# A block-local attention and a token/channel mixer in one kernel: the order in segment 0, batch 1's transposed x, and when later x is loaded

## The chip, the cores and the metric

The kernel runs on one core of a Trainium2 chip. The metric is the time of one execution on the device, in microseconds (us), as the median of several runs. Three runs of the kernel before took 849.24, 851.77 and 852.95 us, with a median of 851.77.

Five engines work side by side, each through its own queue of instructions, in order: TensorE (PE: matmuls, with its weight loads shown apart as PEld), VectorE (DVE), ScalarE (ACT), GpSimd (POOL) and SyncE (SP), which here only issues the transfers (DMAs). An instruction that must wait holds up all that stands behind it in its queue.

## The reference

For 8 batches with 8 heads, 576 tokens and a head size of 64, an attention within chunks of 64 tokens makes x, and a mixer works on it:

```
s = 1/sqrt(64) * q_chunk @ k_chunk^T
p = exp(s - max(s)); p = p / (sum(p) + 1e-9)
x = (p @ v_chunk), heads side by side        # 8 x 576 x 512

h = relu(x^T @ w_tok1) @ w_tok2              # 576 -> 256 -> 576, over tokens
u = x + h^T
out = u + relu(u @ w_ch1) @ w_ch2            # 512 -> 1536 -> 512, over channels
```

The four weights arrive as 64-bit floating-point numbers, and all else is float32.

## The kernel before

**Layout.** The mixer's channel part works with channels on the 128 partitions and tokens on the free axis. Eight batches of 576 tokens make 4608 columns, cut into nine blocks of N = 512 columns. Block k (k = 0 to 8) thus holds the last 64·k columns of batch k-1 and the first 512-64·k of batch k. The attention works with tokens on the partitions, in tiles of 128 tokens: nine tiles for a pair of batches, where the fifth is shared half and half by the two. So x has to be transposed on its way into a block.

**Precision.** A matmul operand is split into a high part and a low part in a reduced float32 format (F32R), and each product takes three matmuls (high·high, low·high, high·low). This is why names come in pairs: `xh`/`xl` for x, `uh`/`ul` for a block of u, `gh`/`gl` for the hidden layer behind the relu, `rh`/`rl` for the token layer behind its relu.

**Weights.** There are 29 weight pieces: 5 of the token mix, then `c1` and `c2` pieces of the channel mix, 12 each. Each is fetched as raw 64-bit words (`raw`, 512 KB for a channel piece, L116) and converted on the chip. ACT makes two reads of the words (L133, L134, issued by `prepare()`, which also fetches the raw words three pieces ahead) and a cast to the high part `kept` (L205); DVE does the rest: clamp, sign, shift, add, and the split of the low part (L211). `convert(n)` takes n **conversion steps** from this list; a channel piece takes five DVE steps. All pieces stay on the chip once they are converted.

**Segments and steps.** The channel mix runs in segments (block, first piece, end): (0, 0..8), (1, 0..12), (0, 8..12), then blocks 2 to 8 over 0..12. Segment 0 is the first of these and does only eight of block 0's twelve pieces, since the weights are still being converted; what it has summed is parked in memory (the part stores and loads). A **step** f does `ch1` (12 matmuls, L556, into one of two PSUM banks `ps_c`), the relu into `gh` on ACT (L564) and `gl` on DVE (L565), and then `ch2` of the step before (12 matmuls into the four sums `acc`, L587).

**Attention.** In some steps (a table sets which: 0, 2, 4 and 6 in segment 0) an `attention` runs. It works on two neighbouring tiles: the older one, whose weights are finished, and the newer one, whose scores begin. In order: ACT copies the older tile's transposed weights `pf` to `pt` (L346); PE makes the newer tile's scores from `qk` (L295) and the older tile's product with `v` (L307), into one tile of two PSUM banks; `qk` and `v` of a later tile are loaded; DVE takes the maximum and subtracts it (L268, L271), ACT takes the exponential `pr` (L275); DVE scales the older product to `x` (L386). Then `pr` is transposed by a way through memory: DVE transposes 32x32 blocks (`blocks`, L318), a store writes them to memory (`far`, L323), and four loads bring them back as `pf` (L329). Last, the older tile's x is split into `xh` and `xl`, and goes the same way as `pr`: one transposition, one `far` store and loads (L329) into `xt`, the transposed x of a block. The loads that belong to a block after the next are put on a list, `late`.

**Start.** The first five tiles (block 0) run ahead of the segments, with matmuls in full float32 and transposes on PE; in front of each tile's next scores stand conversion instructions (`PREPARE`, `FIRST_FILL`).

**Turn.** At the last step in front of a new block ("turn"), PE does `tok1` (two halves, L475, each in a bank of `ps_c`, with relu to `rh`/`rl`), `ch2` of the step before, and `tok2` (L538) for four column blocks m of 128 channels; then DVE adds the transposed x (`u` = sum + `xt`, L543), ACT casts to `uh` (L547), DVE makes `ul` (L548); then comes `ch2` of the last step. Column blocks 0 and 1 take the two banks of `ps_c`, 2 and 3 share one tile of two banks (`two`). At the end of the turn SP issues all `late` loads of x, one after the other.

**What sets the order.** In segment 0 all engines work in the order of the code. From segment 1 on PE and SP keep the order of the code, while ACT and DVE are ordered by a scheduler. SP issues all transfers, in the order of the code.

## Time and profile before

| | |
|---|---|
| median of the runs | 851.77 us |
| profiled execution, its own time | 855.66 us |
| its span (first to last instruction) | 853.7 us |
| granted TensorE clock, mean | 0.967 |
| PE busy | 788.4 us, 92% of the span |
| PEld (weight loads) | 635.6 us, 74% |
| DVE | 378.1 us, 44% |
| ACT | 214.7 us, 25% |
| POOL | 85.6 us, 10% |
| bytes moved | 89.88 MB |

How to read what is quoted below: the page cuts the span into 40 equal slices, and a digit is the busy share of a slice in tenths. In a row of waits stand the engine, the operand and line that waited, the engine, operand and line it waited for, and then total us, number of times and longest. A row of windows has its bounds, its length, and the busy time (with the number of instructions) of PE, PEld, DVE, ACT and POOL, then the granted clock (1 is full speed), the share of DMA time and GB/s. A row of the timeline has the start in us, the duration, the engine, the line and the operation; "x4" are four in a row, counted as one, and the bracket at the end gives how long the engine stood idle before it and for whom. A row with a line number, an operand and "x12" behind two times is the same, cut to one operand.

### The profile page before, as it was taken

The numbers are of one execution on the slowest core, as the hardware profiler recorded it, in microseconds if no ns is written. First come the engines' busy times: TensorE is split into PE (matmuls) and PEld (weight loads), VectorE is DVE, ScalarE is ACT, GpSimd is POOL, SyncE is SP. The second block draws the span as 40 slices with busy tenths as digits, with TensorE's granted clock in tenths as the row PEclk, the third lists the DMA queues.
The fourth block names the chain that finished last, engine by engine and source line by source line (L and its number), as shares of the span: only waits on it lengthen the run. The fifth ranks groups of instructions, "written<-read, shape, count | busy, mean of one in ns | idle before, by whom it ended". The sixth has DMA issues, their size and how long they took to land.

```text
span 853.7 us, 13430 instructions
## 1 busy us (share of the span) xinstructions
PE 788.4 (92%) x5552; PEld 635.6 (74%) x5552; DVE 378.1 (44%) x660; ACT 214.7 (25%) x361; POOL 85.6 (10%) x74
## 2 busy tenths in 40 slices
PE   6885578799999999999999999899999999999998
PEld 4464456688888888878888888778887787887886
DVE  4788784853544433634344334425352324114112
ACT  4545442321231222212322221212211211111010
POOL 0000000200200100211020102100030102003100
PEclk9997789899999999999999999899999999999999
DMA  9636551432452432154315331534043102001001
GB/s 356 233 105 191 186 186 55 136 100 79 145 173 80 132 112 81 66 165 137 112 40 155 110 100 44 167 109 133 27 137 118 51 1 92 1 1 37 13 1 49
DMA packets 67371, 89.88 MB, mean 105 GB/s; under 512 B 7984, under 2 KB 40240, under 8 KB 67312
## 3 DMA queue, kind: packets, MB, share of 16 engines
q1 hardware_dynamic: 67312, 89.05, 31.8%
q8 instruction: 43, 0.70, 0.4%
q14 instruction: 16, 0.13, 0.0%
HBM read 61.10 MB, written 27.00 MB: 103 GB/s over the span
## 4 chain that ended last, share of the span: by engine, by line
PE 79%; DMA 8%; DVE 8%; ACT 3%; issue 1%; SPq 1%; ACTq 0%; DVEq 0%
PE acc L587 33%; PE ps_c L556 30%; PE ps_t L475 5%; PE ps_t L538 5%; DMA raw<-in_wc 3%; DMA far<-blocks 2%; PE ps_sv L307 2%; PE ps_sv L295 2%; DMA v<-in_v 2%; DVE u L543 1%; SPq L329 1%; DVE wtop L150 1%; PE ps_t L517 1%; DMA pf<-far 1%; DVE wtop L157 1%
## 5 line engine op out<-in xcount | busy, mean ns | idle before, releaser
L587 PE MATMUL acc<-gh,kept 128*128 128x512 f32 x864 | 282.0, 408 | 5.0 <-DVE kept L211 5.0
L556 PE MATMUL ps_c<-uh,kept 128*128 128x512 f32 x864 | 270.3, 394 | 0.0
L565 DVE SCALAR_TENSOR_TENSOR gl<-ps_c,gh 128x512 fp32r<-128x512 f32 x108 | 74.6, 691 | 347.9 <-ACT gh L564 347.9
L587 PEld LDWEIGHTS acc<-gh,kept 128*128 128x128 f32 x864 | 165.2, 195 | 42.7 <-DVE kept L211 5.4
L556 PEld LDWEIGHTS ps_c<-uh,kept 128*128 128x128 f32 x864 | 162.9, 189 | 36.9 <-DVE kept L211 0.4
L587 PE MATMUL acc<-gl,kept 128*128 128x512 f32 x432 | 173.6, 402 | 1.6 <-DVE gl L565 1.6
L556 PE MATMUL ps_c<-ul,kept 128*128 128x512 f32 x432 | 169.7, 393 | 0.0
L564 ACT ACTIVATE gh<-ps_c 128x512 fp32r<-128x512 f32 x108 | 64.5, 597 | 316.4 <-PE ps_c L556 316.4
L587 PEld LDWEIGHTS acc<-gl,kept 128*128 128x128 f32 x432 | 83.9, 194 | 21.9 <-DVE gl L565 2.0
L556 PEld LDWEIGHTS ps_c<-ul,kept 128*128 128x128 f32 x432 | 81.5, 189 | 18.8
L404 POOL TENSOR_TENSOR xl<-x,xh 128x512 fp32r<-128x512 f32 x28 | 36.4, 1299 | 456.7 <-ACT xh L403 445.5
L598 POOL TENSOR_TENSOR o<-o,ul 128x512 f32<-128x512 f32 x32 | 43.3, 1383 | 250.2 <-DVE o L596 157.7
L538 PE MATMUL ps_t<-kept,rh 128*128 128x448 f32 (+7 forms) x224 | 49.5, 314 | 6.2 <-DVE u L543 6.2
L307 PE MATMUL ps_sv<-v,pt 64*64 64x64 f32 x992 | 22.3, 232 | 34.9 <-ACT pt L346 34.9
L307 PEld LDWEIGHTS ps_sv<-v,pt 64*64 64x64 f32 x992 | 19.0, 146 | 36.2 <-ACT pt L346 35.9
L538 PEld LDWEIGHTS ps_t<-kept,rh 128*128 128x128 f32 x224 | 37.0, 189 | 9.3 <-DVE u L543 7.8
L275 ACT ACTIVATE pr<-pr 128x512 f32<-128x512 f32 x36 | 22.7, 631 | 68.7 <-DVE pr L271 66.5
L346 ACT COPY pt<-pf 128x512 f32<-128x512 f32 x31 | 19.2, 619 | 74.0 <-DMA pf<-far 71.7
L547 ACT CAST uh<-u 128x512 fp32r<-128x512 f32 x32 | 19.9, 621 | 69.2 <-DVE u L543 69.2
L543 DVE TENSOR_TENSOR u<-ps_t,xt 128x512 f32<-128x512 f32 x32 | 22.0, 689 | 31.9 <-PE ps_t L538 31.7
L475 PE MATMUL ps_t<-xh,kept 128*128 128x512 f32 x112 | 35.0, 393 | 0.0
L538 PE MATMUL ps_t<-kept,rl 128*128 128x448 f32 (+7 forms) x112 | 34.7, 310 | 0.0
(74 smaller groups left out, 606.4 us busy)
## 6 DMA issues: line engine op xcount, KB each, us to landing
qk<-in_qk SPq DMA_DIRECT2D x36, 512.0 KB, 4.3
far<-blocks SPq DMA_DIRECT2D x63, 256.0 KB, 2.1
raw<-in_wc SPq DMA_DIRECT2D x24, 512.0 KB, 5.5
v<-in_v SPq DMA_DIRECT2D x36, 260.0 KB, 4.1
out<-o SPq DMA_DIRECT2D x32, 256.0 KB, 2.0
pf<-far SPq DMA_DIRECT2D x124, 64.0 KB, 2.0
xt<-far SPq DMA_DIRECT2D x96, 64.0 KB, 2.0
xt<-far SPq DMA_DIRECT2D x64, 32.0 KB, 1.8
```

The lines of the kernel that those rows point to most:

```text
L275: nc.scalar.activation(out=pr, in_=pr, func=AF.Exp, scale=1.0 / float(D) ** 0.5)
L307: nc.tensor.matmul(ps[c * CH:(c + 1) * CH, a, (NHP + hp) * D:(NHP + hp + 1) * D], lhsT=t["pt"][a * CH:(a + 1) * CH, hp, c * CH:(c + 1) * C ...
L404: nc.gpsimd.tensor_tensor(out=xl, in0=t["x"], in1=xh.bitcast(F32), op=ALU.subtract)
L475: nc.tensor.matmul(ps, lhsT=lhsT, rhs=rhs, start=(n == 0 and q == 0), stop=(n == len(mt) - 1 and q == len(terms) - 1),)
L538: nc.tensor.matmul(ps[:, at:at + n], lhsT=lhsT[:, cols], rhs=rhs, start=(q == 0), stop=(q == len(terms) - 1),)
L543: nc.vector.tensor_tensor(out=u.rearrange("p (i c) -> p i c", c=BK), in0=ps.rearrange("p (i c) -> p i c", c=BK), in1=xt(k)[:, :, m], op=AL ...
L547: nc.scalar.copy(out=uh[:, m], in_=u)
L556: nc.tensor.matmul(ps, lhsT=weights["c1", f][:, wi, k * P:(k + 1) * P], rhs=u[ui][:, k], start=(k == 0 and q == 0), stop=(k == NDT - 1 and ...
L564: nc.scalar.activation(out=gh, in_=ps, func=AF.Relu)
L565: nc.vector.scalar_tensor_tensor(out=gl, in0=ps, scalar=0.0, in1=gh.bitcast(F32), op0=ALU.max, op1=ALU.subtract)
L587: nc.tensor.matmul(accs[e], lhsT=weights["c2", f][:, wi, e * P:(e + 1) * P], rhs=g[gi], start=(first and q == 0), stop=(end and q == 2),)
L598: nc.gpsimd.tensor_tensor(out=o, in0=o, in1=ul, op=ALU.add)
```

## The change

The arithmetic of x, u and the output stays as it is, except that block 1 gets its x by other matmuls. The change moves and replaces work at these places:

1. *Start.* `PREPARE` goes from two pieces a tile to one, and `END_FILL` from (3, 3, 2) to (3, 2, 2). The first attention takes two conversion steps along. A second identity matrix in F32R, `ident_r`, is made by one ACT cast.
2. *Segment 0, order in a step.* Before, a step ran `prepare` and six conversion steps ahead of its relu and `prepare` and four behind its attention. Now the relu comes first, then the attention, then twice `prepare` and five steps (`STEP_FILL`).
3. *Attention.* The conversion step inside it (one in segment 0) stands ahead of the `far` transposition. `attn_load`, the loads of `qk` and `v`, is moved from right behind the matmuls to behind the `far` store and `pf` loads.
4. *Block 1's x.* At the turn to block 1, x of batches 0 and 1 is added within PSUM by matmuls against an identity matrix, nine for each column block (`tok2` with k == 1). So `u` is the PSUM tile itself, and the three full tiles of batch 1 that are done in segment 0 and only serve block 1 are split, but not stored to `far` or loaded to `xt`. The half tile shared by both batches is stored as before, and loaded later.
5. *PSUM of `tok2`.* Column blocks 0 to 2 use the banks of `ps_c` in turn, and block 3 has the attention's tile alone.
6. *Late x.* The loads of the `late` list are no more issued at the end of the turn, but one by one (four transfers each) at steps 0, 3, 5, 6, 8, 10 and 11 of the next segment (`LATE`), and the shared tile's behind them.
7. One more buffer for `u`, `o` and `back` (5 in place of 4).

```diff
 WARM_T = (6, 2, 0, 0, 0)
 FIRST_FILL = (2, 2, 2, 2, 2)
-PREPARE = (0, 2, 2, 2, 2)
-END_FILL = (3, 3, 2)
-STEP_FILL = (6, 4)
+PREPARE = (0, 1, 1, 1, 1)
+END_FILL = (3, 2, 2)
+STEP_FILL = 5
+LATE = (0, 3, 5, 6, 8, 10, 11)
  
 
...
     ident = const.tile([P, P], F32, name="ident")
     make_identity(nc, ident)
     ctx.enter_context(tc.manual_schedule(engines={nc.sync.engine}))
+    ident_r = const.tile([P, P], F32R, name="ident_r")
+    nc.scalar.copy(out=ident_r, in_=ident)
 
...
                 part = slice(rows.start, rows.start + n * BK)
                 if wait and k > b:
                     late.append((tiles[t]["x"], k, at, n, part))
-                else:
+                elif k > 1:
                     far_in(tiles[t]["x"], xt(k)[:, at:at + n], part)
                 rows = slice(part.stop, rows.stop)
                 first += n
...
             if not n:
                 continue
             terms = []
+            if k == 1:
+                for t, rows, j in mix_tiles(b):
+                    first, end = max(j * P, lo), min(j * P + rows.stop - rows.start, lo + n)
+                    if first >= end:
+                        continue
+                    rows = slice(rows.start + first - j * P, rows.start + end - j * P)
+                    to = ps[:, at + first - lo:at + end - lo]
+                    for x in (tiles[t]["x"],) if b == 0 else (tiles[t]["xh"], tiles[t]["xl"]):
+                        terms.append((to, x[rows, cols], (ident if b == 0 else ident_r)[rows, rows]))
+            to = ps[:, at:at + n]
             for t in range(NT1):
                 if b == 0:
-                    terms.append((rs[b][t], tops["t2", t][:, lo:lo + n]))
+                    terms.append((to, rs[b][t][:, cols], tops["t2", t][:, lo:lo + n]))
                 else:
-                    terms += [(rs[b][t][ri], weights["t2", t][:, wi, lo:lo + n]) for wi, ri in THREE]
-            for q, (lhsT, rhs) in enumerate(terms):
+                    terms += [
+                        (to, rs[b][t][ri][:, cols], weights["t2", t][:, wi, lo:lo + n]) for wi, ri in THREE
+                    ]
+            for q, (to, lhsT, rhs) in enumerate(terms):
                 nc.tensor.matmul(
-                    ps[:, at:at + n], lhsT=lhsT[:, cols], rhs=rhs,
-                    start=(q == 0), stop=(q == len(terms) - 1),
+                    to, lhsT=lhsT, rhs=rhs, start=(q == 0), stop=(q == len(terms) - 1),
                 )
-        u = pool.tile([P, N], F32, tag="o", name="u", bufs=4)
-        nc.vector.tensor_tensor(
-            out=u.rearrange("p (i c) -> p i c", c=BK), in0=ps.rearrange("p (i c) -> p i c", c=BK),
-            in1=xt(k)[:, :, m], op=ALU.add,
-        )
+        u = ps
+        if k > 1:
+            u = pool.tile([P, N], F32, tag="o", name="u", bufs=5)
+            nc.vector.tensor_tensor(
+                out=u.rearrange("p (i c) -> p i c", c=BK), in0=ps.rearrange("p (i c) -> p i c", c=BK),
+                in1=xt(k)[:, :, m], op=ALU.add,
+            )
         nc.scalar.copy(out=uh[:, m], in_=u)
         nc.vector.tensor_tensor(out=ul[:, m], in0=u, in1=uh[:, m].bitcast(F32), op=ALU.subtract)
 
-    def ch1(u, f, fill=0):
+    def ch1(u, f):
         while ("c1", f) not in weights:
             convert(1)
         ps = ps_c1.tile([P, N], F32, tag="c1", name="ps_c1")
...
                     ps, lhsT=weights["c1", f][:, wi, k * P:(k + 1) * P], rhs=u[ui][:, k],
                     start=(k == 0 and q == 0), stop=(k == NDT - 1 and q == 2),
                 )
-        if fill:
-            prepare()
-            convert(fill)
         gh, gl = [pool.tile([P, N], F32R, tag=tag, name=tag) for tag in ("gh", "gl")]
         nc.scalar.activation(out=gh, in_=ps, func=AF.Relu)
         nc.vector.scalar_tensor_tensor(
...
         if j is not None:
             attn_t(j)
         attn_both(i, j)
-        if j is not None and k + 1 < len(order):
-            attn_load(order[k + 1])
         if i is not None:
-            attn_p(i, fill)
+            attn_p(i)
         if j is not None:
             attn_o(j)
+        convert(fill)
         if i is not None:
             attn_far(i)
             attn_z(i)
-        if j is not None:
+        if j is not None and k + 1 < len(order):
+            attn_load(order[k + 1])
+        if j in second[:3]:
+            attn_split(j)
+        elif j is not None:
             attn_end(j)
             for b in range(1, B):
                 if j in [t for t, _, _ in mix_tiles(b)] and (b % 2 == 0 or j % NTILE != 4):
                     attn_x(b, j, wait=True)
 
+    half = []
+
     def ready():
+
         attn_stack(first[4], range(1, 2))
-        tiles[first[4]]["x"] = far_out(tiles[first[4]]["x"], "far_s")
-        attn_x(0, first[4])
+        half.append(far_out(tiles[first[4]]["x"], "far_s"))
 
     def split(i):
         split_high(i)
...
                 half_low.append(half_kept[:, c])
 
     rs, us = {0: r}, {0: block_u()}
-    attention(0)
+    attention(0, 2)
     for m in range(NDT):
         tok2_first(r, m, us[0], ps_acc.tile([P, N], F32, tag="acc", name="ps_t2"))
         convert(END_FILL[2])
     start_ps.close()
-    done, pend, accs = 1, None, []
+    done, pend, accs, owed = 1, None, [], []
     after = None
     for seg, (k, lo, hi) in enumerate(SEGMENTS):
         slots = SLOTS.get((k, lo), SLOTS[3 - (k + 1) % 2] if 2 <= k < B - 1 else ())
...
         if seg == 2:
             after.close()
         for f in range(lo, hi):
-            g = ch1(us[k], f, STEP_FILL[0] if seg == 0 and f < hi - 1 else 0)
+            g = ch1(us[k], f)
             if seg:
                 convert(CONVERT.get((k, lo), 0))
             elif f == 1:
...
                     split(i)
             if (k, f) == (0, NFC - 1):
                 for e in range(NDT):
-                    back = pool.tile([P, N], F32, tag="o", name="back", bufs=4)
+                    back = pool.tile([P, N], F32, tag="o", name="back", bufs=5)
                     nc.sync.dma_start(out=back, in_=part[0, e])
                     part[0, e] = back
             if f - lo in slots:
-                attention(done)
+                attention(done, 1 if seg == 0 else 0)
                 done += 1
             if seg == 0 and f < hi - 1:
-                prepare()
-                convert(STEP_FILL[1])
+                for _ in range(2):
+                    prepare()
+                    convert(STEP_FILL)
             turn = f == hi - 1 and seg + 1 < len(SEGMENTS) and SEGMENTS[seg + 1][1] == 0
             if turn:
                 b = SEGMENTS[seg + 1][0]
...
             pend = (k, us[k], f, g, accs)
             if turn:
                 us[b] = block_u()
-                two = ps_at.tile([P, 2, 512], F32, tag="at", name="ps_t2")
                 for m in range(NDT):
-                    ps = ps_c1.tile([P, N], F32, tag="c1", name="ps_t2") if m < 2 else two[:, m - 2]
+                    if m < 3:
+                        ps = ps_c1.tile([P, N], F32, tag="c1", name="ps_t2")
+                    else:
+                        ps = ps_at.tile([P, 2, 512], F32, tag="at", name="ps_t2")[:, 0]
                     tok2(b, rs, m, us[b], ps)
             if turn or (k, f) == (NB - 1, NFC - 1):
                 ch2(*pend)
                 pend = None
-            if turn:
-                for far, to, at, n, rows in late:
-                    far_in(far, xt(to)[:, at:at + n], rows)
+            if turn and b < B:
+                assert not owed
+                owed = late[:]
                 late.clear()
-            if turn and b == 1:
-                attn_x(1, first[4])
-            if turn and b % 2 == 0 and b + 1 < B:
-                attn_x(b + 1, batch_tiles(b)[-1])
+                if b == 1:
+                    tiles[first[4]]["x"] = half[0]
+                    owed_half = first[4]
+                else:
+                    owed_half = batch_tiles(b)[-1] if b % 2 == 0 and b + 1 < B else None
+            if f - lo in LATE and seg and owed:
+                far, to, at, n, rows = owed.pop(0)
+                far_in(far, xt(to)[:, at:at + n], rows)
+            elif f - lo in LATE and seg and owed_half is not None:
+                attn_x(b if b == 1 else b + 1, owed_half)
+                owed_half = None
     by_hand.close()
```

How this moves instructions, at three places. First **ACT**, from the first step of segment 0 on (`gh<-ps_c` is the relu, `pt<-pf` to `xh<-x` the attention, `wtop`, `low` and `kept` are conversion). Before:

```order
L205 CAST kept_512<-wtop 128x512
L133 ACTIVATE wtop<-raw 128x512
L134 ACTIVATE low<-raw 128x512
L205 CAST kept_512<-wtop 128x512
L564 ACTIVATE gh<-ps_c_607 128x512
L346 COPY pt<-pf 128x4x4x32
L275 ACTIVATE pr<-pr 128x512
L403 CAST xh<-x 128x512
```

Of the change:

```order
L208 CAST kept_490<-wtop 128x512
L577 ACTIVATE gh<-ps_c_598 128x512
L349 COPY pt<-pf 128x4x4x32
L278 ACTIVATE pr<-pr 128x512
L136 ACTIVATE wtop<-raw 128x512
L137 ACTIVATE low<-raw 128x512
L406 CAST xh<-x 128x512
L136 ACTIVATE wtop<-raw 128x512
```

Two readings of raw words and a cast that stood in front of the relu now stand behind the exponential or later; `xh` has a conversion in front of it.

Second **SP**, one attention of segment 0 with the weight loads of its two steps. Before:

```order
L237 DMA qk<-in_qk 128x1024
L242 DMA v<-in_v 128x520
L323 DMA far<-blocks 128x512
L329 DMA pf<-far 32x4x128 x4
L323 DMA far<-blocks 128x512
L329 DMA xt<-far 32x4x128 x4
L116 DMA raw<-in_wc 128x1024 x4
```

Of the change:

```order
L326 DMA far<-blocks 128x512
L332 DMA pf<-far 32x4x128 x4
L240 DMA qk<-in_qk 128x1024
L245 DMA v<-in_v 128x520
L119 DMA raw<-in_wc 128x1024 x4
```

`qk` and `v` moved behind `pf`, and the second `far` store with its loads into `xt` is gone.

Third **PE**, the first column block of `tok2` at the turn to block 1 (the number behind a name tells buffers apart; `r` and `rh`/`rl` are the token layer of batch 0 and 1). Before:

```order
L538 MATMUL ps_t2_1353<-wtop_258,r_517 128x64
L538 MATMUL ps_t2_1353<-wtop_264,r_518 128x64
L538 MATMUL ps_t2_1353<-kept0_512,rh_1315 128x448 x2
L538 MATMUL ps_t2_1353<-kept0_512,rl_1316 128x448
L538 MATMUL ps_t2_1353<-kept0_512,rh_1334 128x448 x2
L538 MATMUL ps_t2_1353<-kept0_512,rl_1335 128x448
```

Of the change:

```order
L553 MATMUL ps_t2_1321<-ident_72,x_480 128x64
L553 MATMUL ps_t2_1321<-wtop_260,r_494 128x64
L553 MATMUL ps_t2_1321<-wtop_323,r_495 128x64
L553 MATMUL ps_t2_1321<-ident_r_79,xh_681 128x128
L553 MATMUL ps_t2_1321<-ident_r_79,xl_682 128x128
L553 MATMUL ps_t2_1321<-ident_r_79,xh_856 128x128
L553 MATMUL ps_t2_1321<-ident_r_79,xl_857 128x128
L553 MATMUL ps_t2_1321<-ident_r_79,xh_1033 128x128
L553 MATMUL ps_t2_1321<-ident_r_79,xl_1034 128x128
L553 MATMUL ps_t2_1321<-ident_r_79,xh_1207 128x64
L553 MATMUL ps_t2_1321<-ident_r_79,xl_1208 128x64
L553 MATMUL ps_t2_1321<-kept0_490,rh_1284 128x448 x2
```

Nine matmuls against the two identity matrices are added to the eight of the token layer.

More of the change, by code (lines that the diff above doesn't have):

```diff
@@ L580, in ch2 @@
             for e in range(NDT):
-                part[k, e] = pool.tile([P, N], F32, tag="o", name="o", bufs=4)
+                part[k, e] = pool.tile([P, N], F32, tag="o", name="o", bufs=5)
                 nc.gpsimd.tensor_tensor(
@@ L593, in ch2 @@
             whole = (k, e) in part
-            o = part.pop((k, e)) if whole else pool.tile([P, N], F32, tag="o", name="o", bufs=4)
+            o = part.pop((k, e)) if whole else pool.tile([P, N], F32, tag="o", name="o", bufs=5)
             uh, ul = (t[:, e].bitcast(F32) for t in u)
```

## The prediction

> **What bounds the kernel now.** I read the page's slices first, then the waits of TensorE (PE) by stretch, then windows and the timeline of the places these name. PE is busy 92% of the span, so at most its idle time, and what it loses at a lower clock, can go.
>
> ```profile
> span 853.7 us, 13430 instructions
> PE   6885578799999999999999999899999999999998
> PE ps_sv L307 <- ACT pt L346: 28.4, 4, 10.2
> PE ps_t L337 <- ACT pr L275: 7.6, 5, 2.5
> PE acc L587 <- DVE kept L211: 5.0, 1, 5.0
> PE acc L587 <- DVE gl L565: 1.6, 1, 1.6
> PE ps_sv L307 <- ACT pt L346: 6.5, 3, 2.8
> PE ps_t L538 <- DVE u L543: 6.2, 7, 1.3
> ```
>
> A slice is 21.3 us: nearly all idle time lies in the first eight, 170 us. The rows below it are PE's waits (total, times, longest). The 28.4 us are the four attentions of segment 0; 6.5 and 6.2 lie behind 200 us, in three attentions and at seven turns. In segment 0 the matmuls on `v` wait for ACT's copy `pt`, and that waits in ACT's queue behind weight conversions, which wait for a weight transfer:
>
> ```profile
> 77.30:100.20 22.90, 14.09 (x113) 11.29 (x114) 17.69 (x35) 10.54 (x19) 1.31 (x1) 0.80 0.71 243
> 100.20:121.10 20.90, 14.56 (x114) 11.64 (x114) 16.69 (x32) 10.16 (x18) 1.29 (x1) 0.83 0.55 187
> 100.19 1.14 PE L307 MATMUL ps_sv<-v,pt 64*64 64x64 f32 x32 [8.78 <-ACT pt L346]
> 104.25 0.33 SPq L323 DMA_DIRECT2D far<-blocks  x1
> 106.29 1.75 SPq L329 DMA_DIRECT2D pf<-far  x4
> 112.83 1.80 SPq L116 DMA_DIRECT2D raw<-in_wc  x4
> 116.68 0.68 ACT L133 ACTIVATE wtop<-raw 128x512 f32<-128x512 f32 x1 [4.37 <-DMA raw<-in_wc]
> 118.31 0.67 ACT L133 ACTIVATE wtop<-raw 128x512 f32<-128x512 f32 x1
> 121.09 1.14 PE L307 MATMUL ps_sv<-v,pt 64*64 64x64 f32 x32 [6.33 <-ACT pt L346]
> ```
>
> The two windows are one pair of steps each (length, then busy time of PE, weight loads, DVE, ACT, POOL, then the granted clock). The loop that sets them: the `v` matmuls end at E = 101.33, `far` is issued at E+2.9, the weights at E+11.5, they land 3.85 later, and 2.8 after the second conversion starts come the next `v` matmuls. DVE, busy 16.7 to 17.7 of it, is a second bound close behind.
>
> **The change part by part.**
>
> *Start: one conversion a tile instead of two, -4.0.*
>
> ```profile
> 17.17 0.74 ACT L133 ACTIVATE wtop<-raw 128x576 f32<-128x576 f32 x1 [2.42 <-DMA raw<-in_w]
> 19.84 0.61 ACT L275 ACTIVATE pr<-pr 128x512 f32<-128x512 f32 x1
> 22.80 0.69 DVE L271 TENSOR_TENSOR pr<-ps_s,mx 128x512 f32<-128x512 f32 x1
> 26.20 0.61 ACT L275 ACTIVATE pr<-pr 128x512 f32<-128x512 f32 x1
> 35.08 0.68 DVE L386 TENSOR_TENSOR x<-ps_v,zi 128x512 f32<-128x512 f32 x1
> ```
>
> The third tile's exp (19.84) stands behind four conversion instructions from 17.17 on; with two it comes at 17.17+1.33 = 18.5, 1.3 earlier. The fourth tile's scores are then ready at 22.80+0.69-1.3 = 22.2 and find ACT free, since the weights that landed at 23.80 are no longer in front: exp at 22.2 for 26.20, so 4.0. Behind that DVE runs without a gap up to the last `x` (35.08), so the 4.0 stay. The conversions left out are made later on DVE and ACT, in segment 0, whose total of 70 steps stays; `ident_r` is one ACT cast ahead of the first weights, which costs nothing.
>
> *Segment 0, relu first, -2.4.*
>
> ```profile
> 51.75 0.69 PE L295 MATMUL ps_sv<-qk 64*64 64x64 f32 x32
> 54.37 0.59 ACT L564 ACTIVATE gh<-ps_c 128x512 fp32r<-128x512 f32 x1
> ```
>
> The first step's relu came 2.6 after its matmuls, behind six conversion steps. Now it follows them, less 0.2 for `ul` of the last column, which is later. For all later steps this is a rotation only: between two relus stand two conversions on ACT before and after, so it ends no wait by itself.
>
> *Segment 0, the loop, -4.6.* Now `far` is issued at E+3.45 (one conversion step of 0.5 goes ahead of the transposition), `pf` 2.04 later, then 1.85 for its four transfers, then `qk` and `v` (0.9), and the weights at E+8.2 in place of E+11.5, because the `far` store and loads of `x` are gone. But `qk` and `v`, 772 KB, now lie ahead of them. What that costs no row of before shows. These two rows bound it:
>
> ```profile
> 95.43 0.66 ACT L133 ACTIVATE wtop<-raw 128x512 f32<-128x512 f32 x1 [5.67 <-DMA raw<-in_wc]
> 97.42 0.67 ACT L133 ACTIVATE wtop<-raw 128x512 f32<-128x512 f32 x1 [0.28 <-DMA raw<-in_wc]
> ```
>
> Two neighbouring weights of 512 KB land 2.0 apart, so 772 KB take 3.0, of which 0.9 passes before the weights are issued: 2.1 more (0 if they share the engines freely, 4.1 at the 187 GB/s of the window above). First weights at E+8.2+3.85+2.1 = E+14.2, the second at E+16.2, next `v` matmuls 2.8 later, 1.1 long: a pair takes 20.1 where it took 22.9 and 20.9, gains of 2.8 and 0.8. The first pair, with four more splits on DVE, is bound by DVE: about 20.8 for 21.8, gain 1.0. DVE loses a transposition of 0.6 and gains a conversion step: nothing. Freed of the weights, a pair could not fall under 16.7 of DVE and the 2 it must wait for PE: at most 2 us more for each.
>
> *First turn, +1.8.*
>
> ```profile
> 257.30 0.39 PE L538 MATMUL ps_t<-kept,rh 128*128 128x128 f32 x2
> 257.64 0.56 PE L538 MATMUL ps_t<-kept,rh 128*128 128x384 f32 x2
> 144.98 0.66 PE L538 MATMUL ps_t<-wtop,r 128*128 128x64 f32 x4 [1.43 <-DVE u L543]
> 152.14 0.80 PE L587 MATMUL acc<-gh,kept 128*128 128x512 f32 x1 [5.00 <-DVE kept L211]
> ```
>
> Three 128-wide matmuls take 0.34, so 0.113 each. Per column block nine of them are added, eight of this kind and one in full float32 at about 0.2: 1.1, and 4.4 for four, all on the path. The 1.43 wait for `u` goes. The 5.0 wait for the second weight of the last block goes down to what stands on DVE then: the last cast 0.62, `ul` 0.69, one split 0.68 and 0.1 between, 2.1; that is -2.9. New is a wait of the second half of tok1 for the bank of the last relu, since ten conversion steps now precede that relu on DVE where four did: 1.7. Sum 4.4-1.4-2.9+1.7. The Trainium skill ("TensorE: Matmul & The Clock Gate", Part 1) states 55.6 ns from start to start for N = 128 at full clock. By it the added matmuls would cost 2.0 and the sum would be 2.4 lower; the rows show twice that, and I keep the rows.
>
> *Segment 1, -1.6*: the wait for `gl` goes, as two fewer conversion steps are ahead of it on DVE and the weights are issued ahead of the part stores.
>
> *Seven later turns, -6.2.* The row `PE ps_t L538 <- DVE u` is the fourth column's block, which shared a tile with the third; in its own tile it waits for nothing late, and the third finds a bank that was read 0.5 before. `u`, cast and `ul` come earlier by as much.
>
> *Three early attentions, -12.4.*
>
> ```profile
> 540.57 0.38 SPq L323 DMA_DIRECT2D far<-blocks  x1
> 545.21 1.75 SPq L329 DMA_DIRECT2D pf<-far  x4
> 374.32 4.54 PE acc L587 x12
> 550.42 5.22 PE acc L587 x12
> 647.75 4.42 PE acc L587 x12
> 455.03 2.99 PE acc L587 x12
> ```
>
> Behind a turn SP issues up to twenty `x` loads, then `qk`, `v`, then `far`, which lands 4.6 later (2.1 is the page's median), so `pt` is late. With `far` ahead of `qk` and `v` and the loads spread, it is at least 2.5 earlier, as much as the longest of these waits needs but 0.3. Each wait is followed by twelve matmuls at a lower clock: 4.54, 5.22 and 4.42 for about 2.8, or 5.9 in all, which goes with the 6.5. The same page (Part 1) has the clock halve after an idle window of about 3.4 us. By that these waits, under 2.8, would cost no clock and I should count 6.5; the three rows disagree.
>
> *`qk` behind `pf`, +4.2.* This is what `attn_load` costs in its new place. Fourteen attentions of the later segments follow the one before by two steps.
>
> ```profile
> 407.65 0.38 SPq L323 DMA_DIRECT2D far<-blocks  x1
> 411.77 0.69 PE L295 MATMUL ps_sv<-qk 64*64 64x64 f32 x32
> DMA to landing us min/median/max: 3.5/4.3/9.8
> ```
>
> `qk` is issued where `far` of `x` was, 407.65, and wanted at 411.77: 4.12 for a transfer that takes 3.5 at best, 4.3 at the median (last row), plus 0.1. I take 0.3 each; the ends are 0 and, at a landing of 4.8, 0.8 (11 in all). The spread `x` loads stand behind `v` and fit into the 12 us between two attentions.
>
> **Sum:** -4.0-2.4-4.6+1.8-1.6-6.2-12.4+4.2 = -25.2. The profiled execution took 855.66, 2.0 over its span of 853.7: 828.5 and 830.5 after. The median of the runs shown, 851.77, lies 3.9 under the profiled one; from it 826.6, which I forecast.
>
> **Rivals.** *Transfers hold segment 0*: `qk` and `v` delay the weights by 4.1 and no pair gains; the window's 187 GB/s speaks for it, the 243 of the other against it. 826.6+4.6 = 831.2. The Trainium skill ("DMA: Bandwidth & Descriptors", Queues, rings and completion order) says that each DMA engine takes the descriptors of a ring in order. By that rule, the weights wait out both loads; the late `far` at 540.57, behind `qk` and `v`, agrees.
>
> *The early attentions still wait*: the spread loads do not do what they should, because `far` still meets transfers. For it: 8 of 12 loads stay at the turn at 532 us. Against: `qk` and `v` do not. 826.6+12.4 = 839.0.
>
> *Slower: PE starves for `qk`.* If `qk` needs over 5.9 from issue to landing, each of the fourteen attentions waits over 1.7, the shortest wait above that brought the lower clock, and pays 2 more for it: 14 x 3.7 = 52 in place of 4.2, 874. The maximum of 9.8 speaks for it, the median of 4.3 against.
>
> **How the numbers follow.** Forecast 0.55, its better end (DVE alone bounds the pairs, `qk` free, near 816) 0.10, transfers hold segment 0 0.15, early attentions still wait 0.10, slower 0.06, and 0.04 for a mixture near no change. The range runs from 815 (all terms at their good end) to 842 (early attentions still wait, and `qk` a little worse). A measurement of this kernel can tell 0.5%, some 4 us, from no change: faster 0.89, same 0.04, slower 0.07.
>
> **What would show it.** Right: the last `x` of the start at 31, the four `v` matmuls of segment 0 at 49, 70, 90 and 110, the waits for `u` gone, the second turn's `acc` at 143, no lower clock behind 200 us. Wrong: PE waiting for `qk` by over 1 us each, waits for `pt` behind 200 us, pairs of 22 or more, or a stall of PE at tok1's second half of over 4 us.

## The result, and the profile after

The changed kernel took **831.07 us** (median of 4 runs, 829.31 to 831.25) against 852.36 for the kernel before: a ratio of 0.9749 with a 95% interval of 0.9717 to 0.9782. A second series gave 831.93 against 849.81, 0.9798 (0.9773 to 0.9824). So it is 2 to 2.5% faster. The forecast was 826.6, 4.5 lower, and the range of 815 to 842 held the time. The profiled execution took 831.25, at a mean clock of 0.981 (0.967 before). One of the four runs of u_late, below, took 1113.84 us in a slow state of the chip, and its median is given for the other three.

The page of the changed kernel (a slice is 20.7 us now), and PE's waits over the whole span, as total, times and longest:

```profile
span 829.5 us, 13486 instructions
PE   7977789999999999999999999999999999999998
PEclk8988899999999999999999999999999999999999
PE ps_sv L310 <- ACT pt L349: 13.1, 4, 4.7
PE ps_sv L298 <- DMA qk<-in_qk: 6.7, 11, 0.9
PE acc L600 <- DVE kept L214: 6.2, 2, 4.4
PE acc L600 <- DVE gl L578: 1.9, 1, 1.9
```

Behind slice 6 no slice of PE or of its clock is under 9 but PE's last. All waits for `pt` that are left are those of segment 0, 13.1 where they were 28.4; behind 200 us PE waits neither for `pt` nor for `u`. New are eleven short waits for `qk`, and one of 4.4 in segment 0 for the first `c2` piece.

For what follows I cut PE's timeline into four stages: the *start* to the end of the first block's last `tok2` matmul, *segment 0* to the first `tok1` matmul, the *first turn* to the end of its last `tok2` matmul, and the *rest* to the start of the last matmul. From before to after they went from 49.1, 80.1, 17.7 and 702.5 us to 44.3, 71.2, 22.9 and 686.8. The rows in segment 0 and at the turn, from the timeline of the changed kernel:

```profile
48.21 0.69 PE L310 MATMUL ps_sv<-v,pt 64*64 64x64 f32 x32 [0.57 <-ACT pt L349]
69.04 1.13 PE L310 MATMUL ps_sv<-v,pt 64*64 64x64 f32 x32 [4.31 <-ACT pt L349]
88.82 1.13 PE L310 MATMUL ps_sv<-v,pt 64*64 64x64 f32 x32 [4.72 <-ACT pt L349]
107.67 0.69 PE L310 MATMUL ps_sv<-v,pt 64*64 64x64 f32 x32 [3.48 <-ACT pt L349]
124.83 0.43 PE L553 MATMUL ps_t<-ident,x 64*128 64x64 f32 x2
128.21 0.43 PE L553 MATMUL ps_t<-ident,x 64*128 64x64 f32 x2
140.40 0.50 PE L600 MATMUL acc<-gh,kept 128*128 128x512 f32 x1 [1.76 <-DVE kept L214]
```

The `v` matmuls stand 20.8, 19.8 and 18.9 apart, a column block of `tok2` takes 3.38, and the wait for the last piece's low half is 1.76 where it was 5.00.

### The profile page after: what moved, and what is told of

Its sections match the earlier page's. It is cut to its first block, busy times and chain, and to the rows that moved or that the text cites. A ratio compares the mean times of both kernels' runs of the same rounds, so it can differ in the third digit from the quotient of the medians.

```text
span 829.5 us, 13486 instructions
## 1 busy us (share of the span) xinstructions
PE 789.9 (95%) x5592; PEld 636.6 (77%) x5592; DVE 372.0 (45%) x653; ACT 214.9 (26%) x362; POOL 86.0 (10%) x74
## 4 chain that ended last, share of the span: by engine, by line
PE 71%; DMA 13%; DVE 7%; ACT 3%; SPq 3%; issue 2%; ACTq 0%; DVEq 0%
PE acc L600 27%; PE ps_c L572 26%; PE ps_t L553 7%; DMA qk<-in_qk 5%; PE ps_t L478 5%; DMA far<-blocks 3%; SPq L332 3%; DMA raw<-in_wc 2%; DMA xc<-x 2%; PE ps_sv L298 2%; PE ps_sv L310 2%; DVE pr L274 1%; DVE blocks L321 1%; DVE mx L271 1%; ACT pr L278 1%
## 5 line engine op out<-in xcount | busy, mean ns | idle before, releaser
L278 ACT ACTIVATE pr<-pr 128x512 f32<-128x512 f32 x36 | 22.7, 631 | 76.0 <-DVE pr L274 75.0
L310 PE MATMUL ps_sv<-v,pt 64*64 64x64 f32 x992 | 21.6, 225 | 13.1 <-ACT pt L349 13.1
L298 PEld LDWEIGHTS ps_sv<-qk 64*64 64x64 f32 x992 | 17.7, 134 | 18.8 <-PE ps_c L572 12.3
L563 ACT CAST uh<-u 128x512 fp32r<-128x512 f32 x28 | 17.4, 621 | 56.2 <-DVE u L559 56.2
L559 DVE TENSOR_TENSOR u<-ps_t,xt 128x512 f32<-128x512 f32 x28 | 19.3, 688 | 25.6 <-PE ps_t L553 25.2
```

What stands on the lines that cost most here:

```text
L278: nc.scalar.activation(out=pr, in_=pr, func=AF.Exp, scale=1.0 / float(D) ** 0.5)
L298: nc.tensor.matmul(ps[c * CH:(c + 1) * CH, a, hp * CH:(hp + 1) * CH], lhsT=qk[a * D:(a + 1) * D, 0, hp, c * CH:(c + 1) * CH], rhs=qk[a * D ...
L310: nc.tensor.matmul(ps[c * CH:(c + 1) * CH, a, (NHP + hp) * D:(NHP + hp + 1) * D], lhsT=t["pt"][a * CH:(a + 1) * CH, hp, c * CH:(c + 1) * C ...
```

## The experiments

Twelve runs, in three series on two chips (the kernel before had medians of 849.55, 850.36 and 849.81 in them). The first four leave out one part of the change each, the next four another part or two, or put the loads at a third place; then two parts alone are added to the kernel before, and one more order is tried (v_first). The stages are those above, from one profile each; a ratio is to the kernel before, with its 95% interval.

| kernel | median us | ratio | start | segment 0 | first turn | rest |
|---|---|---|---|---|---|---|
| as changed, again | 831.93 | 0.9798 (0.9773-0.9824) | 44.8 | 72.1 | 22.9 | 686.2 |
| u_load | 820.95 | 0.9666 (0.9630-0.9702) | 45.0 | 66.9 | 22.9 | 681.2 |
| u_late | 833.37 | 0.9825 (0.9781-0.9870) | 44.8 | 74.0 | 22.9 | 688.5 |
| u_two | 840.64 | 0.9904 (0.9873-0.9935) | 45.2 | 71.9 | 24.9 | 694.5 |
| u_ident | 840.34 | 0.9889 (0.9846-0.9931) | 45.4 | 86.6 | 16.0 | 686.6 |
| u_relu | 838.81 | 0.9862 (0.9840-0.9884) | 45.9 | 77.4 | 22.8 | 688.1 |
| u_start | 835.86 | 0.9828 (0.9805-0.9850) | 49.5 | 72.5 | 22.9 | 685.3 |
| u_loadlate | 827.51 | 0.9745 (0.9714-0.9776) | 45.0 | 65.0 | 22.9 | 688.2 |
| n_between | 820.05 | 0.9646 (0.9628-0.9665) | 45.4 | 67.9 | 22.9 | 678.2 |
| b_load | 860.54 | 1.0130 (1.0111-1.0150) | 50.2 | 88.9 | 17.7 | 698.3 |
| b_ident | 850.16 | 1.0007 (0.9987-1.0026) | 50.2 | 72.8 | 25.2 | 696.2 |
| v_first | 818.30 | 0.9636 (0.9619-0.9652) | 45.7 | 64.7 | 23.0 | 678.3 |

**As changed, again.**

> The changed kernel once more, beside the others of this call: every theory expects 831 within 2 us. It shows how far segment 0, which took 71.2 us in its profile, varies from one profile to the next with the same order; the runs that leave segment 0 as changed gave 71.9 to 74.0.

It came to 831.93, with 72.1 in segment 0. So where a kernel leaves the order in segment 0 alone, that stage was seen at 71.2 to 74.0, and a difference under 3 there says nothing.

**u_load: the loads of `qk` and `v` at their old place.**

```diff
         attn_both(i, j)
+        if j is not None and k + 1 < len(order):
+            attn_load(order[k + 1])
...
             attn_z(i)
-        if j is not None and k + 1 < len(order):
-            attn_load(order[k + 1])
```

> The changed kernel (831.1 us) with the loads of qk and v put back right behind the matmuls of an attention, all else as changed. Theory A (the new place of the loads is what lets the early attentions off): with qk and v ahead of far again, far lands late behind the turns, the waits for pt behind 200 us come back (6.5 us and 5.9 us of lower clock), while the eleven waits for qk (6.7 us) go: 831.1 + 12.4 - 6.7 = 837. Theory B (spreading the x loads is enough): no wait for pt behind 200 us, the 6.7 us for qk go, 824; segment 0 the same within 2 us in both.

820.95: nearly theory B, and more. The waits for `qk` are gone, and of the waits for `pt` behind a turn three are left, 2.4 in all and 1.84 at most. The rest is 5.6 shorter, and segment 0, which both theories had the same within 2, is 4.3 shorter too. Why segment 0 is shorter, SP's and ACT's timelines show for the second attention, first as changed, then with the loads put back:

```profile
73.50 0.33 SPq L326 DMA_DIRECT2D far<-blocks  x1
75.56 1.75 SPq L332 DMA_DIRECT2D pf<-far  x4
77.41 0.38 SPq L240 DMA_DIRECT2D qk<-in_qk  x1
77.88 0.38 SPq L245 DMA_DIRECT2D v<-in_v  x1
78.31 2.08 SPq L119 DMA_DIRECT2D raw<-in_wc  x4
84.41 0.66 ACT L136 ACTIVATE wtop<-raw 128x512 f32<-128x512 f32 x1 [4.47 <-DMA raw<-in_wc]
```

```profile
74.28 0.33 SPq L326 DMA_DIRECT2D far<-blocks  x1
76.32 1.75 SPq L332 DMA_DIRECT2D pf<-far  x4
78.12 1.85 SPq L119 DMA_DIRECT2D raw<-in_wc  x4
80.01 0.61 SPq L240 DMA_DIRECT2D qk<-in_qk  x1
82.24 0.68 ACT L136 ACTIVATE wtop<-raw 128x512 f32<-128x512 f32 x1 [1.49 <-DMA raw<-in_wc]
```

At its new place `qk` and `v` are ahead of the weights, and these reach ACT 84.41-78.31 = 6.1 after their issue; at the old place `qk` comes behind them, and it is 82.24-78.12 = 4.1. The weights follow `far` by 4.8 and by 3.8.

**u_late: all late loads of x at the turn again.**

```diff
-                owed = late[:]
+                for far, to, at, n, rows in late:
+                    far_in(far, xt(to)[:, at:at + n], rows)
                 late.clear()
...
```

> The changed kernel (831.1 us) with all late loads of x issued at the turn again, all else as changed. Theory A (qk and v behind far are enough): the three early attentions do not wait, the time stays at 831 within 2 us. Theory B (the spread loads are what counts, since far stands behind up to twenty loads on SP): waits for pt of 2 to 3 us behind the turns to blocks 3, 5 and 6 and a lower clock behind them, 6 to 12 us: 837 to 843.

833.37, which is 2.3 and 1.4 more than the two medians of the changed kernel. In the profile, of a run of 836.45, segment 0, which the edit doesn't touch, is 2.8 longer, and the rest 1.7. Behind the turns PE waits for `qk`, by 2.7 at most, and not once for `pt`. That is nearer to theory A: with `far` ahead of `qk` and `v` the loads at the turn cost little.

**u_two: column blocks 2 and 3 in one tile again.**

```diff
+                two = ps_at.tile([P, 2, 512], F32, tag="at", name="ps_t2")
                 for m in range(NDT):
-                    if m < 3:
...
+                    ps = ps_c1.tile([P, N], F32, tag="c1", name="ps_t2") if m < 2 else two[:, m - 2]
...
```

> The changed kernel (831.1 us) with column blocks 2 and 3 of tok2 in one tile of two banks again. My theory: at the seven later turns PE waits for u before the fourth column block, 6.2 us in all, and about 1.4 at the first turn for uh and ul: 831.1 + 6.2 + 1.4 = 838.7. Rival (the wait only moves, since ch2 behind it waits for the same ul): less than 2 us more, 831 to 833.

840.64, which is 9.6 and 8.7 more than the two medians of the changed kernel, where my theory gave 7.6. PE's waits for `u` and `ul` behind 120 us:

```profile
PE ps_t L553 <- DVE u L559: 6.4, 7, 1.4
PE ps_t L553 <- DVE ul L564: 1.4, 1, 1.4
```

These are the seven waits of the later turns and the one of the first, by the sizes expected, 7.8 in all. At the first turn more is lost than the 1.4: from 142.00 to 148.40, behind it and the wait for the last piece, PE's granted clock is 0.56, and from the first `tok1` matmul to the next `ch1` it takes 31.2 where the changed kernel, at full clock there, takes 27.6.

**u_ident: block 1's x through memory again.**

```diff
-                elif k > 1:
+                else:
                     far_in(tiles[t]["x"], xt(k)[:, at:at + n], part)
...
-            if k == 1:
+            if k < 0:
...
-        if k > 1:
+        if k > 0:
             u = pool.tile([P, N], F32, tag="o", name="u", bufs=5)
...
-        if j in second[:3]:
-            attn_split(j)
-        elif j is not None:
+        if j is not None:
...
```

> The changed kernel (831.1 us) with block 1 getting its x by stores and loads through memory again, so without the 36 matmuls against an identity. My theory: the first turn gets 6.8 us shorter (3.37 against 1.67 a column block by the two traces), a wait for u of 1 us comes back, and the three pairs of segment 0 get longer since the weights are issued about 4 us later behind the x stores and loads: 2 to 3 us each. Sum 831.1 - 5.8 + 7.5 = 833, between 829 and 835. Rival (segment 0 is bound by DVE, the weights come early enough anyway): pairs of 20.5 or less, 825 to 827.

840.34, more than either theory: the turn is 6.9 shorter as expected, of which 3.0 are lost again right behind it, with a wait of 3.57 for the last piece in place of 1.76; but segment 0 is 15.4 longer, not 7.5. SP's timeline in the second attention:

```profile
78.45 0.33 SPq L326 DMA_DIRECT2D far<-blocks  x1
...
83.25 0.37 SPq L245 DMA_DIRECT2D v<-in_v  x1
83.71 0.40 SPq L326 DMA_DIRECT2D far<-blocks  x1
88.23 1.75 SPq L332 DMA_DIRECT2D xt<-far  x4
90.02 1.85 SPq L119 DMA_DIRECT2D raw<-in_wc  x4
```

The `far` store of x now stands behind `qk` and `v`. SP goes on only when it has landed, 4.5 later (the `far` of `pr`, with nothing ahead of it, takes 2.1 above), and so the weights are issued 11.6 after the `far` of `pr` at 78.45, 6.8 later than as changed. This is what I had not seen: each of the two parts changes what the other is worth. Without the identity matmuls, the moved loads hold up the store of x.

**u_relu: the old order of a step in segment 0.**

```diff
+        if fill:
+            prepare()
+            convert(fill)
         gh, gl = [pool.tile([P, N], F32R, tag=tag, name=tag) for tag in ("gh", "gl")]
...
-                for _ in range(2):
-                    prepare()
-                    convert(STEP_FILL)
+                prepare()
+                convert(4)
```

> The changed kernel (831.1 us) with segment 0's steps in the old order: one piece prepared and six conversion steps ahead of the relu, one piece and four steps behind the attention; all else as changed. My theory (a rotation but for the first relu): 831.1 + 2.4 = 833.5, with the four v matmuls each 2 to 3 us later and no pair longer. Rival (the order shortens every pair, since relu and pt no longer wait behind a weight's transfer): each of the three pairs longer by 2 us or more, 838 or above.

838.81, the rival's time, but not its rows:

```profile
53.85 0.80 PE L310 MATMUL ps_sv<-v,pt 64*64 64x64 f32 x32 [4.62 <-ACT pt L349]
73.44 1.13 PE L310 MATMUL ps_sv<-v,pt 64*64 64x64 f32 x32 [7.18 <-ACT pt L349]
92.73 1.13 PE L310 MATMUL ps_sv<-v,pt 64*64 64x64 f32 x32 [4.60 <-ACT pt L349]
115.39 1.14 PE L310 MATMUL ps_sv<-v,pt 64*64 64x64 f32 x32 [7.52 <-ACT pt L349]
```

Counted from the end of the start, the first `v` matmuls come 4.0 later than as changed (53.85-45.9 against 48.21-44.3). Two pairs are shorter than as changed (19.6 and 19.3), the third is 22.7. Segment 0 takes 77.4, which is 3.4 to 6.2 more than the 71.2 to 74.0 seen with the new order, and 4.0 of it lie in the first step. Why the third pair is long I don't know.

**u_start: two pieces prepared for each of the first tiles again.**

```diff
-PREPARE = (0, 1, 1, 1, 1)
-END_FILL = (3, 2, 2)
+PREPARE = (0, 2, 2, 2, 2)
+END_FILL = (3, 3, 2)
```

> The changed kernel (831.1 us) with two pieces prepared for each of the first tiles again and one more conversion step at the end of the start; all else as changed. My theory: the start is longer by 4 to 4.8 us, and segment 0 as long as it was: 835 to 836. Rival (the pieces prepared early are missing later, so that the new wait of 4.4 us for the first c2 piece goes and gives it back): 831 to 832.

835.86, with a start of 49.5 and a segment 0 of 72.5: my theory. The 4.4 wait for the first `c2` piece falls to 2.8, and segment 0 gets no shorter by it. The wait of 1.76 for the last piece at the first turn goes, and from the first `tok1` matmul to the next `ch1` it takes 25.6 for 27.6, so some 2.0 come back there.

**u_loadlate: both cures of the early attentions undone.** The edits of u_load and u_late together.

> The changed kernel with two parts undone: the loads of qk and v right behind the matmuls again, and all late x loads at the turn again. With the first alone undone the time was 820.95 us, with the second alone 834.9, and in neither did PE wait for pt behind a turn by over 2 us. Theory A (each of the two is enough to free far behind the turn, so the waits come back only where both are undone): 821 + 12.4 = 833. Theory B (the waits of before had another cause, such as the x stores and loads of segment 0 or the tile that two column blocks shared): 821 to 823.

827.51 where u_load had 820.95, and the rest is 688.2 where it was 681.2: theory A, with 7.0 for the 12.4. But u_load has 2.4 of such waits itself; against n_between below, which has none behind the turns and a rest of 678.2, it is 10.0. SP behind the turn to block 5, and PE's wait:

```profile
509.84 6.82 SPq L332 DMA_DIRECT2D xt<-far  x12
516.77 0.36 SPq L240 DMA_DIRECT2D qk<-in_qk  x1
517.23 0.38 SPq L245 DMA_DIRECT2D v<-in_v  x1
517.71 0.38 SPq L326 DMA_DIRECT2D far<-blocks  x1
522.84 1.76 SPq L332 DMA_DIRECT2D pf<-far  x4
526.91 1.13 PE L310 MATMUL ps_sv<-v,pt 64*64 64x64 f32 x32 [3.19 <-ACT pt L349]
```

SP spends 6.8 on loads of x, then `far` lands 5.1 after its issue behind `qk` and `v`. With the loads of x spread (u_load) the wait at this place is 1.84; with `far` ahead of `qk` and `v` (u_late) PE doesn't wait for `pt` there. There are four such waits here, 6.0 in all, and only the one of 3.19 was followed by a lower clock.

**n_between: `qk` and `v` between the `far` store and the `pf` loads.**

```diff
-            attn_far(i)
-            attn_z(i)
+            far = far_out(tiles[i]["pr"])
         if j is not None and k + 1 < len(order):
             attn_load(order[k + 1])
+        if i is not None:
+            tiles[i]["pf"] = pool.tile([P, 4, NHP, BK], F32, tag="pf", name="pf", bufs=1)
+            far_in(far, tiles[i]["pf"])
+            attn_z(i)
```

> The changed kernel with qk and v loaded between the far store and the pf loads, so about 3.9 us earlier in the later segments than as changed, still behind far. Theory A (the waits of PE for qk are the price of the new place, and SP's wait for far has room for the two loads): the eleven waits for qk go, behind the first turn it is as fast as the run with the loads at the old place, and only segment 0's weights still stand behind qk and v: 831.1 - 5.6 = 825.5. Theory B (pf then shares the transfers with qk and v and lands late): waits for pt of about 1 us at most attentions, 831 or more.

820.05: theory A, and 5 better than it gave, the same as u_load within the intervals of the two. No wait for `qk` nor for `pt` is left behind the first turn. In segment 0, SP issues the two loads while it waits for `far` anyway:

```profile
74.58 0.33 SPq L326 DMA_DIRECT2D far<-blocks  x1
75.00 0.38 SPq L240 DMA_DIRECT2D qk<-in_qk  x1
75.47 0.40 SPq L245 DMA_DIRECT2D v<-in_v  x1
76.82 1.75 SPq L332 DMA_DIRECT2D pf<-far  x4
78.61 1.93 SPq L119 DMA_DIRECT2D raw<-in_wc  x4
```

`pf` follows `far` by 2.2 (2.1 as changed), and the weights by 4.0 in place of 4.8.

**b_load: the kernel before with the loads of `qk` and `v` moved, and nothing else.** The edit is the reverse of u_load's.

> The kernel before (about 850.5 us) with one part of the change alone: qk and v loaded behind the pf loads. My theory: in segment 0 the far store of x now stands behind 772 KB, SP waits 4.7 us for it in place of some 2, and holds up the weights, 6 us or more for the segment, as in the run without the identity matmuls; later the early attentions gain 7.0 and the waits for qk cost 5.6. Sum 850.5 + 6.5 - 1.4 = 855.6. Rival (the terms as predicted: early attentions 12.4, qk 4.2, weights 2.1 a pair at most): 850.5 - 12.4 + 4.2 + 4.2 = 846.5.

860.54, slower than the kernel before by 1.3%, and 5 more than my theory. PE's waits over the span:

```profile
PE ps_sv L307 <- ACT pt L346: 35.7, 4, 12.2
PE ps_sv L295 <- DMA qk<-in_qk: 7.4, 10, 2.2
```

The early attentions no longer wait, since the four waits for `pt` are all in segment 0, but those rose from 28.4 to 35.7, and segment 0 from 80.1 to 88.9. The terms as I had predicted them (846.5) are off by 14.

**b_ident: the kernel before with block 1's x by identity matmuls, and nothing else.** The edit is the change's in `tok2`, `attn_x`, `ready` and behind `attn_z`, with `ident_r`.

> The kernel before (about 850.5 us) with one part of the change alone: block 1's x by identity matmuls, so no x stores and loads in segment 0. My theory: the weights are issued about 4 us earlier after each attention, the three pairs of segment 0 get 3 to 4 us shorter each until DVE bounds them, about 11 in all, and the first turn longer by 6.8 less a wait of 1.4 for u: 850.5 - 11 + 5.4 = 845. Rival (the gain needs the new order too, since ACT still waits for weights ahead of pt): segment 0 shorter by 5 at most, 850 or more.

850.16, no change (ratio 1.0007). Segment 0 fell by 7.3, and the turn rose by 7.5: there `two` is left, so the matmuls wait another 1.4 for `ul`. It is the rival's time, and lies between the two in segment 0 (11 and 5 at most). The 7.3 need no new order; what u_ident lost beyond them, some 8, is about the 8.8 that b_load adds: the hold-up behind `qk` and `v`. In b_load's trace, too, the `far` store of x behind them holds SP for 4.3 and 4.6 (from 91.22 to 95.48 and from 115.18 to 119.73); in the same places of the kernel before it was 2.1 and 2.9.

**v_first: as n_between, and in segment 0's attention steps ten conversion steps ahead of the softmax.**

```diff
         attn_both(i, j)
+        for _ in range(fills):
+            prepare()
+            convert(STEP_FILL)
         if i is not None:
             attn_p(i)
...
-            if seg == 0 and f < hi - 1:
+            if seg == 0 and f < hi - 1 and f not in slots:
```

> The changed kernel with qk and v between far and pf (820.05 us), and in segment 0's attention steps the two weight pieces prepared and their ten conversion steps taken right behind the attention's matmuls, ahead of its softmax, far store and pf loads. Theory A (segment 0 is set by when SP issues the weights, behind far and pf): the weights are issued some 7 us earlier in a pair, the wait of 4.5 us for the first c2 piece goes, and pairs fall to what DVE is busy, 16 to 17 us: 820 - 4.5 - 3 = 812.5. Theory B (DVE is already the bound, the order does not matter): 818 to 821.

818.30, the lowest of all, though its interval overlaps that of n_between, and 6 short of theory A. Two pairs of steps (window, length, busy PE, weight loads, DVE, ACT, POOL, clock), and a wait of the first pair:

```profile
70.90:87.50 16.60, 13.81 (x120) 11.08 (x112) 16.39 (x35) 10.99 (x20) 1.29 (x1) 0.91 0.57 197
87.50:103.10 15.60, 13.69 (x120) 10.96 (x112) 15.50 (x31) 9.65 (x17) 1.30 (x1) 0.91 0.58 187
63.73 1.13 PE L298 MATMUL ps_sv<-qk 64*64 64x64 f32 x32 [4.96 <-DMA qk<-in_qk]
```

The later pairs fell to what DVE is busy, 16.4 of 16.6 and 15.5 of 15.6: there the transfers bound nothing any more. In the first pair the 4.5 wait for the `c2` piece went, and one of 5.0 for `qk` came, as `far` and with it `qk` now stand behind ten conversion steps.

## Why the prediction was right, and where it was off

**Start, -4.0:** right, by 0.8 too small. The last `x` moved from 35.08 to 30.28, 4.8.

**Relu first, -2.4:** right in kind, too small. u_relu gives 4.0 us for the first step.

**The loop of segment 0, -4.6:** right in kind, too small. The first pair was to take 20.8 and the next 20.1 each; they took 20.8, 19.8 and 18.9, which are gains of 1.0, 3.1 and 2.0, 6.1 in all. Segment 0 with the relu fell by 8.9 for 7.0, although the wait of 4.4 for the first `c2` piece, which I had not foreseen, is in it. `qk` and `v` ahead of the weights cost 2.0 at the one place shown, for 2.1 predicted, and 4.3 in all by u_load. What I had not seen is that the same loads also hold up the `far` store of x: with the loads moved and that store back in place (u_ident) the segment takes 86.6, more than the 80.1 of before. So the identity matmuls are worth 15 us there with the loads at their new place, and 7.3 with the loads at the old one. The Trainium skill ("DMA: Bandwidth & Descriptors", Queues, rings and completion order) has each engine take a ring's descriptors in order; the 6.1 against 4.1 of u_load and the 4.5 of u_ident agree with it.

**First turn, +1.8:** from the first `tok1` matmul to the next `ch1` it took 27.3 before and 27.6 after. The step that was mis-sized is the nine matmuls at 1.1 a column block: a block takes 3.38 for 1.67, 1.7 each. The eight in F32R take 1.13 where I had 0.9, the one in full float32 0.37 where I had 0.2, and the eight of the token layer 0.2 more than before. The wait for the last piece is 1.76 (2.1 predicted), and the clock behind it stays full (1.00, where it was 0.64 before), which I had left out. The 1.7 at tok1's second half didn't come.

**Segment 1, -1.6:** wrong. The wait for `gl` is still there, 1.9 for 1.6; why isn't shown.

**Later turns, -6.2:** right, by the 6.4 of the seven waits that come back in u_two.

**Early attentions, -12.4:** the mechanism is right, and the use made of this term is what left the forecast 4.5 too low. The 12.4 was read from one execution, of 855.66 us, and for that execution it holds: the spans of the two profiles differ by 24.2, and the other terms as measured leave 10.5 to 13.5 of it for this one (an estimate, with 5.6 or 8.6 for the moved loads, below). From 855.66 the sum gave 830.5, and the profiled execution of the change took 831.25. But I took the whole sum off the median of 851.77, although part of what that execution had over the median, 3.9, may have been these very waits. For that speaks b_ident, which shares the order behind the first turn and whose profiled execution, 850.50, lies near its median: its rest is 696.2 where the profile of before had 702.5. The three waits of 1.66, 2.76 and 2.09 are 0.77, 2.52 and 0.67 in it, and only the 2.52 is followed by a lower clock. What these waits would come to in a second profile of the kernel before is open. I had also named two cures for these waits together. By u_late, `far` ahead of `qk` and `v` is enough to end them; by u_load, the spread loads leave 2.4.

**`qk` behind `pf`, +4.2:** right in kind, too small; the waits add up to 6.7, and the rest is 5.6 longer than with the loads at the old place (u_load), and 8.6 longer than in n_between. With the 4.3 in segment 0 this part of the change costs 10 us against u_load, and buys no more than the 2.4 of waits for `pt` that the spread loads leave there, which n_between ends without the cost.

So the sum came near also because its errors partly cancel: segment 0 and the first turn came out better than forecast, segment 1 and the loads of `qk` worse.

Of the rivals, *PE starves for `qk`* failed since its waits stayed at 0.9 at most, too short to bring a lower clock (in the second series at 1.3 at most; no wait up to 1.41 brought one in any run, last section). *The early attentions still wait* failed: behind 200 us PE waits not once for `pt`. *Transfers hold segment 0* has the time that lies nearest, 831.2 for the 831.07 measured, but by chance: by it no pair gains, and they gained 6.1, while the moved loads cost 4.3 there.

## What to carry to other kernels

When a transfer is moved on a queue that works in order, look at what now stands behind it, above all at a store whose landing the queue itself waits for: the place between a store and the loads that must wait for it cost nothing here, the place ahead of the store did. Where a change has two cures for one wait, take each away alone before both are kept; here the one that was dearer cost 10 us. And a wait that varies from run to run is to be priced from more than one profile, or scaled to the median.

## What the runs showed of the hardware that was not expected

Whether PE's clock falls behind a wait isn't settled by the length of the wait alone. Waits in two runs, u_late and u_load, and behind each the eight `acc` matmuls with `gh`, of the twelve of a step (ns min/median/max, first and last start):

```profile
401.52 0.69 PE L298 MATMUL ps_sv<-qk 64*64 64x64 f32 x32 [1.67 <-DMA qk<-in_qk]
L600 PE MATMUL acc<-gh,kept x8: 389/389/497, 402.6 to 405.0; 128*128 128x512 f32 x8
```

```profile
524.71 1.09 PE L310 MATMUL ps_sv<-v,pt 64*64 64x64 f32 x32 [1.84 <-ACT pt L349]
L600 PE MATMUL acc<-gh,kept x8: 392/513/793, 525.7 to 529.3; 128*128 128x512 f32 x8
```

After 1.67 the clock stayed full (granted 1.00 from 402.00 to 405.50), after 1.84 it didn't (0.66 from 525.50 to 529.50); but the 1.66 of the kernel before at 373.6 brought the 4.54 that the prediction quotes. Over all waits of the attention's matmuls in the fourteen profiles, take the time from the start of the waiting matmuls to that of the eighth row behind them in the timeline. It is 3.25 to 3.30 after each of the 93 waits up to 1.41 with no other wait close behind, and 4.67 or more after each of the 49 from 2.30 on. Of the eight between, from 1.66 to 2.17, four stayed at 3.3 and four went to 4.8. So a wait of some 2 us costs PE either itself alone or 1.5 more. The Trainium skill ("TensorE: Matmul & The Clock Gate", Part 1) speaks of an idle window of about 3.4 us; these rows show a lower clock after half of that.
